# One float32 copy of the first MLP's result between two MLP stages, and a scheduler that counts overwritten inputs

## The chip, the core and the metric

The program runs on one core of a Trainium2 chip. The metric is device microseconds (us) of the whole program, from its start to its end. The engines are named as the profile names them: PE multiplies matrices (PEld loads its weights), DVE, ACT and POOL work on vectors, SP issues the DMAs.

## What is computed

Three layers follow one another. First a gated linear attention with a complex decay, then an MLP with a rational activation, then eight expert MLPs whose outputs are weighted by a Sinkhorn-normalised gate. Only the last result is an output.

```python
x = attention(q, k, v, a_re, a_im)             # 4 x 8 heads x 768 steps x 48, then reshaped to 3072 x 384
h = x @ w_in                                   # first MLP: 384 -> 2048
g = (a0 + a1*h + a2*h*h + a3*h*h*h) / (1 + |b0|*|h| + |b1|*h*h + 1e-6)
x = g @ w_out                                  # 2048 -> 384
P = sinkhorn(exp(x @ w_gate))                  # 3072 x 8
out = sum over e of P[:, e] * (relu(x @ w1[e]) @ w2[e])   # second MLP, 8 experts of 384 -> 1024 -> 384
```

## The kernel before

**Two parts.** In the first part attention and first MLP are interleaved; the page of the profile puts nearly all of it on line 302, where the scheduler issues each operation. In the second part the experts run over the 3072 tokens (PE lines 672 to 674 and 1044 to 1046). A last branch with the general fallback is not taken with these inputs.

**First part.** Attention is cut into 13 pieces (`PIECES`, p = 0 to 12). For each piece `attn_normalise` makes the decays (`n`, `an`), `attn_prefix` the running products (tiles `u`, `tot`, `x`, `f1a`, `f2a`, `ex`; each of four shifts `sh` is a matmul that waits for the `x` before it), `attn_scale` the scaled keys and queries (`f`, `kq`), which go to DRAM (`kqd`) and come back as `raw`. `attn_unit` and `attn_half` then do 24 blocks of 128 tokens on PE (`t`, `sc`, `u`, `y`). The first MLP takes the tokens in 12 blocks of 256 (m = 0 to 11), its 2048 channels in 8 groups (gi): `moe1_first` makes `h` on PE and the activation on ACT and DVE (tiles `m`, result `gt`, or `gh` and `gl`), `moe1_second` adds up `x2` in PSUM.

**Precision by parts.** A float32 matrix product is done as three fast products: a value is split into a rounded part `hi` (type fp32r) and the rest `lo`, and hi*hi, hi*lo and lo*hi are added.

**Between the MLPs.** At the end of a block, `moe1_second` splits `x2` chunk by chunk (three of 128 x 256): ACT (seldom DVE) writes `hi`, DVE writes `lo`, and a DMA of both goes to the DRAM tensor `x2g`. `x2_load` reads 512 tokens of it into a tile `xb` that holds both parts, with one DMA each. Tiles `xb0` to `xb3` take the SBUF space of attention and are loaded when the last block of attention is done; `xb4` and `xb5` are loaded as the second part starts.

**What sets the order.** Every operation is an `Op` with a cost; `Either` lists the engines that may do it (`g.tt`: POOL or DVE; `g.cpa`: ACT, DVE or POOL). The `Schedule` picks, at build time, the operation that could start first by its model, and among those of an engine the one with the lowest key, a due time made of the constants `PITCH`, `GROUP`, `OU`, `OB`, `OA`, `ON`, `OW`, `OS`, `SH`, `HHD`, `WS`. `PRICE` weighs a choice of engine by its cost. An operation with `port` set also waits for a common resource `PORT`: those of POOL with an input in SBUF, and those of DVE with more than one such input. `x is not self.out` leaves an input out of this count where it is also the output. Each engine then works its list in order, so an operation that waits holds up all behind it on its engine.

Of the kernel before, what the change touches and what calls it, by code (L numbers as in the profile page):

```python
# [8 lines left out]
F32 = mybir.dt.float32  # L9
# [9 lines left out]
NT = B * S  # L19
# [42 lines left out]
PLAIN = 'FFFSSFFS'  # L62
SMP = 'DD'

PITCH = 63.96
GROUP = 6.92
OU = 52.54
OB = 77.92
OA = 199.64
ON = 97.15  # L70
OW = 45.47
OS = 27.91
SLACK = 0
HHD = 2.39
SH = (-2.5, 31.7, -15.0, 20.1, 3.1, -26.5, 4.2, 13.7, 4.0, 12.5, -36.2, -58.5, 17.9)
WS = 1.91
PRICE = {'DVE': 1.0, 'POOL': 0.05, 'ACT': -0.18}
LAT = {'PE': 0.2, 'ACT': 0.145, 'DVE': 0.13, 'POOL': 0.075, 'SP': 1.0}
TS = True

# [12 lines left out]
class Op:  # L93


    def __init__(self, eng, fn, args, kw):
        self.eng, self.fn, self.args, self.kw = eng, fn, args, kw
        self.deps = []
        self.out = kw["out"] if "out" in kw else args[0]
        ap = [x for k, x in [*enumerate(args), *kw.items()] if k not in ("out", "accum_out", "op", "func") and hasattr(x, "tensor")]  # L100
        self.ins = [x for x in ap if x is not self.out]
        n = int(np.prod(self.out.shape[1:]))
        ps = any(x.space == PSUM for x in self.ins)
        name = fn.__name__

        sb = sum(x.space != PSUM and int(np.prod(x.shape[1:])) > 1 for x in self.ins)
        self.port = sb > 0 and (eng == "POOL" or eng == "DVE" and (sb > 1 or not ps and name in ("tensor_scalar", "tensor_copy")))
        ptr = sum(hasattr(kw.get(k), "tensor") for k in ("scale", "bias", "accum_out", "scalar")) + (
            name == "tensor_scalar" and sum(hasattr(x, "tensor") for x in args[2:4]))
        self.lat = LAT[eng]  # L110
        if eng == "PE":
            f32 = args[1].dtype != F32R
            two = f32 and not kw.get("is_transpose")
            self.cost = (1 + two) * max(n * (1 + f32) / 2400, 0.108) + 0.013 * (not f32)
            if two:
                self.cost = {32: 0.076, 96: 0.162}.get(self.out.shape[0], self.cost)
        elif eng == "ACT":
            self.cost = (0.05 if ps else 0.092) + n * 0.836e-3 + 0.0935 * ptr
        elif eng == "DVE":
            one = name == "tensor_scalar" and not ps  # L120
            self.cost = ((n / 2 if one else n) + 65) / 960 + 0.061 * ptr
        elif eng == "POOL":
            c = {"tensor_tensor": 2.1, "tensor_scalar": 1.18, "affine_select": 0.9}.get(name, 0.8)
            self.cost = (0.15 if c > 0.8 else 0.04) + c * n * 1e-3
        else:
            self.cost = 0.06
# [709 lines left out]
def moe1_second(g, m):  # L836

    v, act, pool, pe, sync = g.eng
    kw = {"skip_group_check": True}
    for gi in range(NG):  # L840
        yield lambda: (m, gi) in g.gs and (2 * gi, 1) in g.w1 and (2 * gi + 1, 1) in g.w1
        yield m * PITCH + gi * GROUP + OS
        gh, gl = g.gs.pop((m, gi))
        if m not in g.sums:
            g.sums[m] = yield New(g.ps_x, [128, 4, TK], keep=True, tag="x2", name=f"x2_{m}")
        x2 = g.sums[m]
        for f in range(2):
            ff = 2 * gi + f
            w = g.w1[ff, 1]
            for c in range(3):  # L850

                st, sp = ff == 0 and c != 1, ff == NF - 1
                if plain(ff):
                    yield pe.matmul(x2[:, c], w[:, 0, c], gh[:, f], start=st, stop=sp, **kw)
                    continue
                yield [
                    pe.matmul(x2[:, c], w[:, 0, c], gh[:, f], start=st, stop=False, **kw),
                    pe.matmul(x2[:, c], w[:, 1, c], gh[:, f], start=False, stop=False, **kw),
                    pe.matmul(x2[:, c], w[:, 0, c], gl[:, f], start=False, stop=sp, **kw),
                ]  # L860
            if m == NT // TK - 1:
                g.free(w)
        g.free(gh, *([gl] if gl is not None else []))
    for k in range(3):
        x = yield New(g.wraw, [128, 2, TK], F32R, tag="raw", name=f"x2s{m}_{k}")
        sc = g.co[:, 11:12]
        yield Either(act.activation(x[:, 0], x2[:, k], AF.Identity, scale=sc), v.tensor_scalar(x[:, 0], x2[:, k], sc, None, MULT))
        yield v.scalar_tensor_tensor(out=x[:, 1], in0=x2[:, k], scalar=sc, in1=x[:, 0].bitcast(F32), op0=MULT, op1=SUB)
        yield sync.dma_start(
            out=g.x2g[:, k, :, m * TK:(m + 1) * TK].rearrange("l p t -> p l t"), in_=x.bitcast(F32)  # L870
        )
        g.free(x)
    g.free(x2)
    g.done.add(("S", m))

# [364 lines left out]
def general_moe1(g):  # L1240
# [6 lines left out]
    with tc.For_i(0, NT, 128) as t0:  # L1247
        x = tmp.tile([128, DM], F32, tag="gx", name="gx")
        sync.dma_start(out=x, in_=g.yg[bass.ds(t0, 128), :])
        xt = tmp.tile([128, 3, 128], F32, tag="gxt", name="gxt")  # L1250
        for k in range(3):
            p = ps.tile([128, 128], F32, tag="gt", name=f"gtp{k}")
            pe.matmul(p, x[:, k * 128:(k + 1) * 128], g.cst[:, 0], is_transpose=True, start=True, stop=True)
            act.copy(xt[:, k], p)
        acc = [pa.tile([128, 128], F32, tag=f"ga{c}", name=f"ga{c}") for c in range(3)]
        for f in range(NF):
            p = ps.tile([128, 128], F32, tag="gh", name=f"ghp{f}")
            for k in range(3):
                pe.matmul(p, w[2 * f][:, k], xt[:, k], start=k == 0, stop=k == 2)
            h, s, u, z, za, n, d = (tmp.tile([128, 128], F32, tag=f"gm{i}", name=f"gm{i}_{f}") for i in range(7))  # L1260
            act.copy(h, p)
            act.activation(za, p, AF.Abs)
            v.tensor_scalar(s, za, 1.0, None, ALU.max)
            v.reciprocal(u, s)
            v.tensor_tensor(out=z, in0=h, in1=u, op=MULT)
            v.tensor_tensor(out=za, in0=za, in1=u, op=MULT)

            v.tensor_scalar(n, z, co[:, 3:4], None, MULT)
            v.scalar_tensor_tensor(out=n, in0=u, scalar=co[:, 2:3], in1=n, op0=MULT, op1=ADD)
            v.tensor_tensor(out=n, in0=n, in1=z, op=MULT)  # L1270
            v.tensor_tensor(out=d, in0=u, in1=u, op=MULT)
            v.scalar_tensor_tensor(out=n, in0=d, scalar=co[:, 1:2], in1=n, op0=MULT, op1=ADD)
            v.tensor_tensor(out=n, in0=n, in1=z, op=MULT)
            v.tensor_tensor(out=z, in0=d, in1=u, op=MULT)
            v.scalar_tensor_tensor(out=n, in0=z, scalar=co[:, 0:1], in1=n, op0=MULT, op1=ADD)

            v.tensor_scalar(d, d, C1, None, MULT)
            v.tensor_tensor(out=u, in0=u, in1=za, op=MULT)
            v.scalar_tensor_tensor(out=d, in0=u, scalar=co[:, 4:5], in1=d, op0=MULT, op1=ADD)
            v.tensor_tensor(out=za, in0=za, in1=za, op=MULT)  # L1280
            v.scalar_tensor_tensor(out=d, in0=za, scalar=co[:, 5:6], in1=d, op0=MULT, op1=ADD)
            v.reciprocal(d, d)
            v.tensor_tensor(out=n, in0=n, in1=d, op=MULT)
            v.tensor_tensor(out=n, in0=n, in1=s, op=MULT)
            for c in range(3):
                pe.matmul(acc[c], w[2 * f + 1][:, c], n, start=f == 0, stop=f == NF - 1)
        for c in range(3):
            xs = tmp.tile([128, 2, 128], F32R, tag="gxs", name=f"gxs{c}")
            act.copy(xs[:, 0], acc[c])
            v.tensor_tensor(out=xs[:, 1], in0=acc[c], in1=xs[:, 0].bitcast(F32), op=SUB)  # L1290
            sync.dma_start(out=g.x2g[:, c, :, bass.ds(t0, 128)].rearrange("l p t -> p l t"), in_=xs.bitcast(F32))
    g.close("gpa", "gps", "gt", "gm")


def x2_load(g, t):
# [1 line left out]
    per = TB // TK  # L1297
    yield lambda: all(("S", t * per + i) in g.done for i in range(per))
    xt = yield New(g.px[t], [128, 2, 3, TB], F32R, keep=True, tag=f"x{t}", name=f"xb{t}")
    for l in range(2):  # L1300
        yield g.eng[4].dma_start(
            out=xt[:, l].bitcast(F32), in_=g.x2g[l, :, :, t * TB:(t + 1) * TB].rearrange("k p t -> p k t")
        )
    g.x2[t] = xt


# [19 lines left out]
def kernel_body(tc, g):  # L1326
# [22 lines left out]
    dp = opn("dram", space=bass.MemoryType.DRAM)  # L1349
    g.dkq = opn("dkq", 3, space=bass.MemoryType.DRAM)  # L1350
    g.xt = {}
    g.x2g = dp.tile([2, 3, 128, NT], F32, name="x2g")
    g.yg = dp.tile([NT, DM], F32, name="yg")
    g.kq, g.w1, g.we, g.an, g.ex, g.qk, g.gs, g.state, g.carry = ({} for _ in range(9))
    g.done = set()
# [132 lines left out]
```

## Time and profile before

| | |
|---|---|
| median of 3 runs | 2522.71 us (2521.58 to 2524.64) |
| profiled execution | 2521.8 us, of which 2519.8 us is the span from first to last instruction |
| PE busy in the span | 2328.5 us (92%), 13921 matmuls |
| DVE busy | 1201.0 us (48%) |
| ACT busy | 854.1 us (34%) |
| POOL busy | 483.8 us (19%) |
| first matmul of the experts | at 866.7 us |
| granted PE clock over the span | 0.977 of full |

A share over the whole span says little here: the first 867 us and the rest have different limits, and the change lies in the first part and at the seam. Rows are read by stretch.

### The profile page before, as it was taken

To read this page: it belongs to the slowest core of one execution; us is meant where nothing else is said; L and a number is where in the kernel's file an instruction comes from. 1 tells how busy PE (TensorE), PEld (TensorE's weight loads), DVE (VectorE), ACT (ScalarE), POOL (GpSimd) and SP (SyncE) were. 2 spreads that over 40 slices of the span, in tenths; PEclk is the share of its full clock that TensorE was granted. 3 is DMA by queue.
4 is the path that set the end of the run, shared out by engine and by line. 5 is a ranking of instruction groups with operands and counts; after the bars stand their busy time and mean duration, and the time that the engine had idled before them with its cause. 6 is when DMAs were issued, how large, how long until landed. Compare 5 with 4: busy or idle time off the path is not lost.

```text
span 2519.8 us, 34763 instructions
## 1 busy us (share of the span) xinstructions
PE 2328.5 (92%) x13921; PEld 2098.6 (83%) x13921; DVE 1201.0 (48%) x2295; ACT 854.1 (34%) x1741; POOL 483.8 (19%) x537
## 2 busy tenths in 40 slices
PE   1477898988999999999999999999999999999998
PEld 0366788877889978989999989998999999999998
DVE  6899988888987614442252233224222221222222
ACT  3467676766667621221121121121112112112111
POOL 3356444454441000020020020010011002001000
PEclk9888999999999999999999999999999999999999
DMA  3543332333322520030030021012001001000000
GB/s 99 154 126 95 108 107 82 101 90 94 108 89 70 200 64 1 1 94 1 1 100 1 1 71 31 1 39 63 1 13 38 1 1 51 1 1 20 26 25 27
DMA packets 141837, 138.18 MB, mean 55 GB/s; under 512 B 32481, under 2 KB 126689, under 8 KB 141665
## 3 DMA queue, kind: packets, MB, share of 16 engines
q1 hardware_dynamic: 141664, 135.86, 17.7%
q8 instruction: 111, 1.82, 0.3%
q14 instruction: 62, 0.50, 0.1%
HBM read 102.80 MB, written 33.03 MB: 54 GB/s over the span
## 4 chain that ended last, share of the span: by engine, by line
PE 74%; DVE 11%; DMA 6%; issue 3%; POOL 3%; ACT 3%; SPq 1%; POOLq 0%; DVEq 0%; ACTq 0%
PE ye L1044 10%; PE ye L1045 10%; PE ye L1046 10%; PE he L673 10%; PE he L672 10%; PE he L674 10%; PE x L302 4%; DVE m L302 3%; PE h L302 3%; DVE f L302 1%; DMA ai<-in_a_im 1%; ACT m L302 1%; PE t L302 1%; PE sc L302 1%; DVE n L302 1%
## 5 line engine op out<-in xcount | busy, mean ns | idle before, releaser
L1032 DVE SCALAR_TENSOR_TENSOR lo<-he,hi 128x512 fp32r<-128x512 f32 x384 | 265.4, 691 | 1104.5 <-ACT hi L1031 1104.5
L1031 ACT ACTIVATE hi<-he 128x512 fp32r<-128x512 f32 x384 | 229.7, 598 | 1207.6 <-PE he L674 1059.1
L302 DVE SCALAR_TENSOR_TENSOR m<-m,co,m 128x512 f32<-128x512 f32 x192 | 165.5, 894 | 18.7 <-ACT m L302 18.5
L302 ACT ACTIVATE m<-m,co 128x512 f32<-128x512 f32 x192 | 137.4, 719 | 1.4
L302 PE MATMUL t<-cst_sb,raw 128*96 128x128 f32 x384 | 66.5, 304 | 35.6 <-DMA raw<-kqd 33.7
L1057 DVE SCALAR_TENSOR_TENSOR acc<-ye,skp,acc 128x384 f32<-128x384 f32 x168 | 92.2, 611 | 5.7 <-PE ye L1046 2.4
L302 PEld LDWEIGHTS t<-cst_sb,raw 128*96 128x96 f32 x384 | 48.1, 141 | 43.3 <-issue 29.0
L302 DVE SCALAR_TENSOR_TENSOR m<-m,co,h 128x512 f32<-128x512 f32 x96 | 70.7, 738 | 12.9 <-ACT m L302 12.7
L302 ACT ACTIVATE m<-h 128x512 f32<-128x512 f32 x96 | 56.3, 587 | 41.2 <-PE h L302 40.2
L302 PE MATMUL sh<-tot,cst_sb 128*128 128x96 f32 x26 | 8.0, 403 | 64.2 <-POOL tot L302 45.6
L302 ACT COPY tt<-t 96x512 f32<-96x512 f32 x95 | 54.7, 577 | 37.0 <-PE t L302 36.5
L302 ACT ACTIVATE m<-h,co 128x512 f32<-128x512 f32 x96 | 65.3, 680 | 4.2 <-DVE gl L302 1.6
L302 PE MATMUL sc<-tt,tt 96*128 96x128 f32 x384 | 56.2, 291 | 6.0 <-ACT tt L302 5.2
L302 PEld LDWEIGHTS sh<-tot,cst_sb 128*128 128x128 f32 x26 | 5.5, 265 | 66.6 <-POOL tot L302 46.4
L302 ACT ACTIVATE m<-m 128x512 f32<-128x512 f32 x96 | 60.0, 626 | 1.1
L302 PEld LDWEIGHTS sc<-tt,tt 96*128 96x128 f32 x384 | 49.2, 200 | 11.5 <-ACT tt L302 7.7
L302 DVE SCALAR_TENSOR_TENSOR gt<-m,m 128x512 f32<-128x512 f32 x60 | 46.4, 774 | 0.3
L302 ACT ACTIVATE n<-n,bias 128x384 f32<-128x384 f32 x72 | 43.9, 610 | 5.6 <-DVE n L302 3.6
L302 DVE TENSOR_TENSOR f<-an,ex 128x384 f32<-128x384 f32 x70 | 45.5, 665 | 0.0
L302 POOL TENSOR_TENSOR x<-u,u 128x48 f32<-128x48 f32 x62 | 31.6, 526 | 44.6 <-DVE u L302 37.8
L302 POOL TENSOR_TENSOR f<-an,ex 128x384 f32<-128x384 f32 x26 | 32.5, 1256 | 30.7 <-DVE kq L302 10.0
L302 POOL TENSOR_TENSOR kq<-an,f 128x384 f32<-128x384 f32 x21 | 29.9, 1423 | 43.8 <-DVE f L302 26.3
(1329 smaller groups left out, 7018.1 us busy)
## 6 DMA issues: line engine op xcount, KB each, us to landing
rawe<-in_moe_w SPq DMA_DIRECT2D x128, 192.0 KB
kqd<-kq SPq DMA_DIRECT2D x48, 384.0 KB
raw<-kqd SPq DMA_DIRECT2D x48, 384.0 KB
x2g<-x2s SPq DMA_DIRECT2D x36, 256.0 KB
xb<-x2g SPq DMA_DIRECT2D x12, 768.0 KB
raw<-in_moe_w_in SPq DMA_DIRECT2D x48, 128.0 KB
raw<-in_moe_w_out SPq DMA_DIRECT2D x16, 384.0 KB
rawc<-in_moe_w_in SPq DMA_DIRECT2D x16, 384.0 KB
```

The costliest lines, as they stand in the source:

```text
L302: ins = op.fn(*op.args, **op.kw)
L672: pe.matmul(out, w[0], x[0], start=start, stop=False, **kw),
L673: pe.matmul(out, w[0], x[1], start=False, stop=False, **kw),
L674: pe.matmul(out, w[1], x[0], start=False, stop=stop, **kw),
L1031: act.activation(hi, ps, AF.Relu)
L1032: v.scalar_tensor_tensor(out=lo, in0=ps, scalar=0.0, in1=hi.bitcast(F32), op0=ALU.max, op1=SUB)
L1044: pe.matmul(ys[j], hi[:, c], wh, start=f == 0, stop=False)
L1045: pe.matmul(ys[j], hi[:, c], wl, start=False, stop=False)
L1046: pe.matmul(ys[j], lo[:, c], wh, start=False, stop=f == NFE - 1)
L1057: v.scalar_tensor_tensor(out=acc, in0=ys[j], scalar=g.P[:, i, e:e + 1], in1=acc, op0=MULT, op1=ADD)
```

## The change

The block sum `x2` is scaled once into a float32 tile of 128 x 768 by one operation and stored by one DMA of 384 KB; `x2g` has half the size. `x2_load` loads one float32 copy of 768 KB into the `lo` half of the tile, ACT rounds it into the `hi` half (128 x 1536), and POOL or DVE subtracts in place. The count behind `port` takes every input that lies in SBUF, the overwritten ones too. Ten constants of the scheduler have other values, in the list `SH` two entries. The fallback branch is changed in the same way.

```diff
-PITCH = 63.96
-GROUP = 6.92
-OU = 52.54
+PITCH = 63.56
+GROUP = 6.1
+OU = 62.81
...
-OA = 199.64
+OA = 254.69
...
-OW = 45.47
-OS = 27.91
+OW = 55.28
+OS = 26.46
...
-HHD = 2.39
-SH = (-2.5, 31.7, -15.0, 20.1, 3.1, -26.5, 4.2, 13.7, 4.0, 12.5, -36.2, -58.5, 17.9)
-WS = 1.91
-PRICE = {'DVE': 1.0, 'POOL': 0.05, 'ACT': -0.18}
+HHD = 2.09
+SH = (-2.5, 31.7, -15.0, 20.1, 3.1, -26.5, 4.2, 13.7, 9.8, 12.5, -32.7, -58.5, 17.9)
+WS = 2.46
+PRICE = {'DVE': 1.0, 'POOL': 0.12, 'ACT': -0.18}
...
-        sb = sum(x.space != PSUM and int(np.prod(x.shape[1:])) > 1 for x in self.ins)
+        sb = sum(x.space not in (PSUM, DRAM) and int(np.prod(x.shape[1:])) > 1 for x in (ap if "out" in kw else ap[1:]))
...
-    for k in range(3):
-        x = yield New(g.wraw, [128, 2, TK], F32R, tag="raw", name=f"x2s{m}_{k}")
-        sc = g.co[:, 11:12]
-        yield Either(act.activation(x[:, 0], x2[:, k], AF.Identity, scale=sc), v.tensor_scalar(x[:, 0], x2[:, k], sc, None, MULT))
-        yield v.scalar_tensor_tensor(out=x[:, 1], in0=x2[:, k], scalar=sc, in1=x[:, 0].bitcast(F32), op0=MULT, op1=SUB)
-        yield sync.dma_start(
-            out=g.x2g[:, k, :, m * TK:(m + 1) * TK].rearrange("l p t -> p l t"), in_=x.bitcast(F32)
-        )
-        g.free(x)
+    x = yield New(g.wraw, [128, 3, TK], tag="raw", name=f"x2s{m}")
+    sc = g.co[:, 11:12]
+    yield Either(act.activation(x, x2[:, :3], AF.Identity, scale=sc), v.tensor_scalar(x, x2[:, :3], sc, None, MULT))
+    yield sync.dma_start(out=g.x2g[:, :, m * TK:(m + 1) * TK].rearrange("k p t -> p k t"), in_=x)
+    g.free(x)
...
-    for l in range(2):
-        yield g.eng[4].dma_start(
-            out=xt[:, l].bitcast(F32), in_=g.x2g[l, :, :, t * TB:(t + 1) * TB].rearrange("k p t -> p k t")
-        )
+    raw = xt[:, 1].bitcast(F32)
+    yield g.eng[4].dma_start(out=raw, in_=g.x2g[:, :, t * TB:(t + 1) * TB].rearrange("k p t -> p k t"))
+    yield g.eng[1].copy(xt[:, 0], raw)
+    yield g.tt(xt[:, 1], raw, xt[:, 0].bitcast(F32), SUB)
```

The scheduler therefore deals out the first part anew. Counted over its whole list (line 302), POOL has 217 operations where it had 421, DVE 1627 where it had 1471, ACT 1036 where it had 1040. 204 operations leave POOL on balance: 191 of attention and of splits go to DVE, 13 copies to ACT. DVE loses the 38 operations of the split of `x2`, gains 4 subtractions of 128 x 1536, and gives one copy to ACT. By width, the 191 are 47 of 384 columns, 61 of 192, 60 of 48, and 23 of other widths.

The first place is POOL's list at the prefix of piece 6 (`an6` are its decays; `u`, `tot` and `x` its running products), before:

```order
L302 TENSOR_TENSOR u1_6_3562<-an6_2148 128x96
L302 TENSOR_TENSOR u2_6_3563<-an6_2148 128x96
L302 TENSOR_TENSOR tot_6_3538<-u1_6_3562,u2_6_3563 128x48
L302 TENSOR_TENSOR tot_6_3538<-u1_6_3581,u2_6_3582 128x48 x2
L302 TENSOR_TENSOR u1_6_3601<-an6_2148,tot_6_3538 128x96
L302 COPY vtail1_143<-v5_1_3547 128x2x4x16
L302 TENSOR_TENSOR an7_2954<-ar7_0_3397,n3_7_0_3418 128x8x48
L302 TENSOR_TENSOR x_6_3640<-u1_6_3638,u2_6_3639 128x48 x2
L302 COPY gtail0_144<-g5_0_3544 96x2x4x16
L302 TENSOR_TENSOR x_6_3784<-u1_6_3782,u2_6_3783 128x48 x2
```

And POOL's list at the same place now:

```order
L302 TENSOR_TENSOR u1_6_3673<-an6_2077 128x96
L302 TENSOR_TENSOR an7_2858<-ar7_0_3469,n3_7_0_3487 128x8x48
L302 TENSOR_TENSOR x_6_3808<-u1_6_3806,u2_6_3807 128x48 x2
L302 TENSOR_TENSOR n1_7_1_3757<-n1_7_1_3757,n2_7_1_3758 128x384
L302 TENSOR_TENSOR x_6_3895<-u1_6_3893,u2_6_3894 128x48 x2
L302 TENSOR_TENSOR n1_7_1_3757<-n1_7_1_3757,n3_7_1_3759 128x384
```

The running products `tot` and two copies have left POOL, which now has two operations of the next piece's normalisation between the steps of this one.

The second place is DVE's list around the end of block 9 (`x2_9` is its sum, `m1`, `m2` and `gt` are the activation of block 10), before:

```order
L302 SCALAR_TENSOR_TENSOR m2_10_1_8711<-m2_10_1_8711,co_141,h10_1_8676 128x512
L302 SCALAR_TENSOR_TENSOR x2s9_0_8737<-x2_9_8257,co_141,x2s9_0_8737 128x256
L302 SCALAR_TENSOR_TENSOR x2s9_1_8751<-x2_9_8257,co_141,x2s9_1_8751 128x256
L302 SCALAR_TENSOR_TENSOR m1_10_1_8710<-m1_10_1_8710,co_141,m3_10_1_8712 128x512
L302 SCALAR_TENSOR_TENSOR m2_10_1_8711<-m2_10_1_8711,co_141,m3_10_1_8712 128x512
L302 SCALAR_TENSOR_TENSOR x2s9_2_8763<-x2_9_8257,co_141,x2s9_2_8763 128x256
L302 SCALAR_TENSOR_TENSOR gt10_1_8777<-m1_10_1_8710,m2_10_1_8711 128x512
```

And DVE's list there now:

```order
L302 TENSOR_TENSOR kq12_3_8559<-an12_6620,f2_12_8492 128x4x96
L302 SCALAR_TENSOR_TENSOR m1_10_0_8578<-m1_10_0_8578,co_141,m3_10_0_8580 128x512
L302 SCALAR_TENSOR_TENSOR m2_10_0_8579<-m2_10_0_8579,co_141,m3_10_0_8580 128x512
L302 SCALAR_TENSOR_TENSOR m2_10_1_8636<-m2_10_1_8636,co_141,h10_1_8581 128x512
L302 SCALAR_TENSOR_TENSOR gt10_0_8651<-m1_10_0_8578,m2_10_0_8579 128x512
L302 SCALAR_TENSOR_TENSOR m1_10_1_8635<-m1_10_1_8635,co_141,m3_10_1_8637 128x512
L302 SCALAR_TENSOR_TENSOR m2_10_1_8636<-m2_10_1_8636,co_141,m3_10_1_8637 128x512
```

The three splits of the sum are gone, and the last operation of attention's preparation (`kq12_3`) stands here, which before stood in block 9, ahead of `m2_9_6`.

The third place is ACT's list after the last block of attention (`xt11` takes its result, `m1`, `m2` and `m3` are the activation of block 10), before:

```order
L302 ACTIVATE m2_10_6_9070<-h10_6_8902,co_141 128x512
L302 CAST xt11_9007<-y23_9026 128x3x128
L302 ACTIVATE m1_10_6_9069<-m1_10_6_9069,co_141 128x512
L302 ACTIVATE m3_10_6_9071<-m1_10_6_9069,co_141 128x512
L302 ACTIVATE m3_10_6_9071<-m3_10_6_9071 128x512
L302 ACTIVATE m1_10_7_9164,hsum_68<-h10_7_9072 128x512
```

And ACT's list there now:

```order
L302 ACTIVATE m2_10_6_8996<-h10_6_8858,co_141 128x512
L302 CAST xb0_9030<-xb0_9030 128x1536
L302 ACTIVATE m1_10_6_8995<-m1_10_6_8995,co_141 128x512
L302 CAST xb1_9031<-xb1_9031 128x1536
L302 ACTIVATE m3_10_6_8997<-m1_10_6_8995,co_141 128x512
L302 ACTIVATE m1_10_7_9069,hsum_68<-h10_7_8998 128x512
L302 ACTIVATE m3_10_6_8997<-m3_10_6_8997 128x512
L302 ACTIVATE m2_10_7_9070<-h10_7_8998,co_141 128x512
L302 CAST xb2_9032<-xb2_9032 128x1536
L302 ACTIVATE m1_10_7_9069<-m1_10_7_9069,co_141 128x512
L302 CAST xb3_9033<-xb3_9033 128x1536
```

Four roundings of loaded tiles now stand between the steps of the activations of groups 6 and 7; DVE has the four subtractions in two pairs at the same place, the first pair after `gt10_5`, the second after `gt10_6`.

## Rows read from the trace of the kernel before

**Rows 1.** Windows: length, busy us of PE, PEld, DVE, ACT, POOL; clock, DMA share, GB/s.

```profile
0.00:130.00 130.00, 38.68 (x278) 32.72 (x279) 99.41 (x277) 55.06 (x132) 44.96 (x56) 0.90 0.43 125
130.00:755.00 625.00, 534.77 (x4552) 484.94 (x4555) 554.76 (x1066) 416.36 (x903) 311.70 (x355) 0.93 0.34 100
755.00:866.60 111.60, 111.54 (x907) 104.22 (x899) 78.53 (x121) 83.16 (x163) 13.27 (x14) 1.00 0.36 118
...
818.00:838.00 20.00, 20.00 (x145) 18.92 (x138) 10.32 (x15) 10.93 (x21) 0.00 (x0) 1.00 0.89 315
```

**Rows 2.** Waits from 130 to 755 us: total, times, longest.

```profile
PE t L302 <- DMA raw<-kqd: 12.1, 7, 2.9
...
PE sh L302 <- POOL tot L302: 7.4, 4, 3.4
...
PE sh L302 <- POOL x L302: 4.0, 3, 2.5
```

**Rows 3.** DVE groups to 880 us: count, busy us, mean ns, idle before.

```profile
L302 DVE SCALAR_TENSOR_TENSOR m<-m,co,m 128x512 f32<-128x512 f32 x192 | 165.5, 894 | 18.7 <-ACT m L302 18.5
L302 DVE SCALAR_TENSOR_TENSOR m<-m,co,h 128x512 f32<-128x512 f32 x96 | 70.7, 738 | 12.9 <-ACT m L302 12.7
...
L302 DVE TENSOR_TENSOR f<-an,ex 128x384 f32<-128x384 f32 x70 | 45.5, 665 | 0.0
L302 DVE SCALAR_TENSOR_TENSOR n<-n,n 128x384 f32<-128x384 f32 x48 | 35.5, 739 | 0.1
...
L302 DVE SCALAR_TENSOR_TENSOR x2s<-x,co,x2s 128x256 fp32r<-128x256 f32 x36 | 17.2, 476 | 6.9 <-ACT x2s L302 6.9
```

**Rows 4.** The same by tile: shortest/median/longest ns, first and last start.

```profile
L302 DVE SCALAR_TENSOR_TENSOR m<-m,co,m x192: 734/750/1776, 128.9 to 866.7; 128x512 f32<-128x512 f32 x192
L302 DVE SCALAR_TENSOR_TENSOR m<-m,co,h x96: 729/736/749, 126.5 to 863.1; 128x512 f32<-128x512 f32 x96
...
L302 DVE TENSOR_TENSOR f<-an,ex x70: 543/548/1639, 49.5 to 758.6; 128x384 f32<-128x384 f32 x70
...
L302 DVE TENSOR_TENSOR an<-f,f x54: 343/346/1152, 50.8 to 759.6; 128x192 f32<-128x192 f32 x54
...
L302 DVE SCALAR_TENSOR_TENSOR n<-n,n x48: 541/552/1364, 17.2 to 691.3; 128x384 f32<-128x384 f32 x48
...
L302 DVE TENSOR_TENSOR tot<-u,u x44: 192/201/1025, 51.7 to 723.6; 128x48 f32<-128x48 f32 x44
```

**Rows 5.** POOL groups to 880 us.

```profile
L302 POOL TENSOR_TENSOR an<-f,f 128x192 f32<-128x192 f32 x42 | 32.9, 787 | 22.4 <-DVE f L302 22.3
...
L302 POOL TENSOR_TENSOR x<-u,u 128x48 f32<-128x48 f32 x62 | 31.6, 526 | 44.6 <-DVE u L302 37.8 <-PE t L302 6.8
L302 POOL TENSOR_TENSOR kq<-an,f 128x384 f32<-128x384 f32 x21 | 29.9, 1423 | 43.8 <-DVE f L302 26.3 <-issue 14.8 <-ACT f L302 2.6
L302 POOL TENSOR_TENSOR an<-f1a,f2a 128x192 f32<-128x192 f32 x30 | 26.9, 905 | 25.9 <-DVE f1a L302 25.6
```

**Rows 6.** Timeline of DVE from 870.9 us: start, us, what.

```profile
871.00 0.55 DVE L302 TENSOR_TENSOR we4o<-rawe,we4o 128x384 fp32r<-128x384 f32 x1
871.47 0.55 DVE L302 TENSOR_TENSOR we5i<-rawe,we5i 128x384 fp32r<-128x384 f32 x1
```

**Rows 7.** Timeline of ACT from 877 us.

```profile
879.88 0.51 ACT L302 CAST we6o<-rawe 128x384 fp32r<-128x384 f32 x1
```

**Rows 8.** Timeline of SP's DMA issues from 760 us.

```profile
818.37 10.08 SPq L302 DMA_DIRECT2D xb<-x2g  x8
```

**Rows 9.** Longest pieces of the chain that ended last: start, us, what.

```profile
306.11 6.61 DMA raw<-kqd
...
772.61 6.91 PE x L302 x48
779.52 2.15 PE h L302 x18
781.67 2.59 PE x L302 x12
```

More of the change, by code (lines that the diff above doesn't have):

```diff
@@ L1287, in general_moe1 @@
         for c in range(3):
[L1288 to L1291, printed above, removed]
+            xs = tmp.tile([128, 128], F32, tag="gxs", name=f"gxs{c}")
+            act.copy(xs, acc[c])
+            sync.dma_start(out=g.x2g[c, :, bass.ds(t0, 128)], in_=xs)
     g.close("gpa", "gps", "gt", "gm")
@@ L1351, in kernel_body @@
     g.xt = {}
-    g.x2g = dp.tile([2, 3, 128, NT], F32, name="x2g")
+    g.x2g = dp.tile([3, 128, NT], F32, name="x2g")
     g.yg = dp.tile([NT, DM], F32, name="yg")
```

## The prediction

> **What bounds the kernel now.** I read the windows first, because the change lies in the first 867 us alone. They show two stretches with different limits [rows 1]. From 130 to 755 us nothing is full: of 625 us DVE is busy 554.8 (89%), PE 534.8 (86%), ACT 416.4, POOL 311.7. From 755 us to the first matmul of the experts PE is busy 111.54 of 111.6 us, DVE 78.5. So the second stretch is a sum of matmuls, and every stall of PE there adds to the time; the first is paced by DVE and by chains that pass through it. The experts behind are PE's work too and keep their program. The waits of the first stretch name DVE and POOL ahead of PE in attention's prefix: its shift matmuls wait 7.4 us for `tot` from POOL and 4.0 for `x` from POOL; transposes wait 12.1 us for loads of `kqd`, which the change doesn't touch [rows 2].
>
> Then I compare DVE's groups by mean and by median, because DVE's 89% is not all work. `m<-m,co,m`, with both tensor inputs in SBUF, takes 894 ns in the mean, 750 in the median and 1776 at most; `m<-m,co,h`, which reads one from PSUM, has the same width and never takes more than 749 [rows 3, 4]. In both of the SBUF-only groups that show it beside it, `n` and `f`, the median is near the shortest and the mean far above it. Some executions of these are stretched, and POOL is what works beside them. The stretch is (894 - 750) x 192 = 27.6 us for `m`, (739 - 552) x 48 = 9.0 for `n`, (665 - 548) x 70 = 8.2 for `f`: 45 us in three groups [rows 3, 4]. The smaller groups, reckoned in the same way, add about 53: some 98 us that DVE loses beside POOL.
>
> **The change, part by part.**
>
> *What DVE gains.* 191 operations come over from POOL. On DVE a 384-wide one lasts 0.55 us, but the next starts 0.47 after it [rows 6], so a place in the list costs 0.08 less than a duration. 47 of 384 columns: 22.1 us. 61 of 192, at 0.346 - 0.08 [rows 4]: 16.2. 60 of 48, at 0.201 - 0.08 [rows 4]: 7.3. The 23 of other widths lie between these, about 0.25 each: 5.8. Together 51 us.
>
> *What DVE loses.* The split's 36 operations of 17.2 us in all [rows 3]; nine of the twelve blocks end before 755 us, so three quarters of it, 12.9 us, fall there. That DVE and ACT no longer take turns over three chunks frees `x2` some 2 us earlier per block, which I count at nothing: PE has other products in its list.
>
> *What POOL's leaving gives back.* Four groups carry most of it [rows 5]: 17 `kq<-an,f` of 1.423 us, 45 `x` of 0.526, 24 `an<-f1a,f2a` of 0.905, 27 `an<-f,f` of 0.787 make 91 us. The other 91 of the 204 I take at 0.8, the mean of these 113: 73. So about 164 of the 357 us that POOL works before 755 (311.7 and 45.0 ahead of 130 [rows 1]) go away, 46%. No row shows DVE beside a POOL half as busy. The floor is that only the three groups above are relieved, 46% of 45 = 21 us; the ceiling is that the new list keeps what is left of POOL clear of DVE, 98 us. I take 46% of 98 = 45, because the loss goes with the time that POOL works: it is absent where an input is in PSUM and where POOL rests.
>
> *Sum for DVE:* 51 - 13 - 45 = -7 us, between +17 and -60. DVE is 89% busy there, so I let it pass one to one.
>
> *Chains.* Half of the 11.4 us in which PE's shifts wait for POOL [rows 2] should go, as `tot` leaves POOL and `x` mostly does (45 of 62). Each step idles DVE too, which waits for the shift. Part of this is in the sum already, so I take -4, between 0 and -8.
>
> *Scheduler.* The constants and the wider `port` decide only the order, and their price is in the counts above. DVE's list reaches the end of attention's preparation (`kq12_3`) some two groups later than before, while the first matmul of attention's last two blocks keeps its place in PE's list, behind the first product of `gt10_0`. PE's products of block 10 ahead of that are the cover; if it were gone, each us that `kq12_3` is late would be one at the end.
>
> *The seam.* Stores and loads halve: SP issues 24 stores and 6 loads fewer, all off the path. New is that ACT rounds `xb0` to `xb3` in the middle of block 10's last two activations, and that each rounding waits for a load. A 1536-wide rounding costs at most four of 384 columns, 2.0 us [rows 7], I take 1.5; a subtraction on DVE at most four of 0.47, 1.9. ACT and DVE are half idle there (10.9 and 10.3 us of 20) [rows 1], so the work fits; the wait is the risk, because ACT and DVE hold `gt10_6` and `gh10_7` behind it, and PE wants those. Before, the first load is issued at 818.4 [rows 8], as attention's last matmul ends. PE then has 12 products of `gt10_2`, 18 of `h10_7` and 48 of groups 3 to 5: 2.59 + 2.15 + 6.91 = 11.7 us [rows 9], so it asks for `gt10_6` at about 830, and for `gh10_7` 4.7 us later. The loads moved 315 GB/s [rows 1]: 0.79 MB is 2.5 us, and no landing is shorter; a load of half the size kept PE's chain 6.6 us [rows 9]. With 4.5 us the first lands at 823. From there ACT needs two roundings and three activations (5 us), DVE two subtractions and four products of the activation (about 6, partly beside it): `gt10_6` at 831.5, some 2 us late, and `gh10_7`, behind two more roundings, another 1 to 2. The price is 3 us, between 0 (2.5 us to land) and 6 (6.6). A rule that bears on it, on the Trainium skill's page "DMA: Bandwidth & Descriptors", section "Anatomy of one DMA", puts a DMA at 2.0 us and its bytes over 436 GB/s, measured on another path of issue; an estimate from that page is 3.8 us for this load, and a seam of 2 us instead of 3. No row of this trace shows the landing of `xb0` by itself.
>
> `xb4` and `xb5` are subtracted on POOL, at four times the shortest 384-wide POOL operations or more, 4 us each and more. Nothing on PE's way waits for them: the gate wants `xb4` some 40 us later.
>
> By the Trainium skill, page "SBUF — State Buffer", section "Who interferes with whom", DVE and GpSimd share one pair of ports under an exclusive lock, so one of them stands still for the whole instruction of the other. The longest `m<-m,co,m` agrees with it: 1776 against 734 ns is one POOL instruction of about 1 us [rows 4]. By this rule the subtractions of `xb4` and `xb5` would each stop DVE's splits of weights for 4 us, a loss that the old kernel doesn't have; DVE's `lo` of the experts reads PSUM and goes on, so the sum stays.
>
> **Total.** 2521.8 us for the profiled execution - 7 - 4 + 3 = 2513.8, and with the first 130 us, where the prefix's first `tot` also leaves POOL, -1: 2512.8. The median of the runs is 0.9 us above the profiled one: I say 2513.
>
> **Rivals.**
>
> *DVE loses more than it gets (slower).* It is the engine nearest to full, and 38 us net come onto it before any relief. If what is left of POOL meets DVE more often, since DVE's list is denser, the relief stays at 21 us, and DVE takes 17 more: 2521.8 + 17 + 3 - 2 = 2540. It decides from a relief under about 35 us, with a chance of 0.25. For it speaks that POOL's parts are not spread evenly: long 384-wide operations stay there; against it, that the chains lose their hops.
>
> *No change.* DVE is relieved, but PE's stretch is held by the loads of `kqd` (12.1 us) and by chains through ACT, and what is won ahead of 755 is waited for again: 2519 to 2526. For it speaks that no engine is above 89%; chance 0.17.
>
> *The new order fits better.* If the list now stands in the order in which things are ready, PE's 90 idle us of the first stretch (625 - 534.8) could fall by a third beyond the sum, with a relief near its ceiling: about 2485. Chance 0.15.
>
> *The forecast,* between 2500 and 2517: 0.43.
>
> **How the numbers follow.** About 0.2% (5 us) is what this measurement can tell from no change. Faster is the forecast and the better order, 0.58; same 0.17; slower 0.25. The range leaves out the far ends of the last two: 2485 to 2537; the likeliest case alone is 2500 to 2517.
>
> **What the new profile would show.** In the stretch up to 755 us POOL at about 170 us and DVE still near 89%; `m<-m,co,m` near 820 ns in the mean with an unchanged median; the waits of `sh` for POOL halved; the tail full but for about 3 us near 830, named as `x` waiting for `gt` or `gh`; the first matmul of the experts at about 858 us. The prediction is wrong if DVE's mean durations don't fall with POOL's time, or if PE waits for an `xb` load for more than 6 us.

## The result and the profile after

The changed kernel takes 2485.38 us (median of 4 runs, 2481.61 to 2488.16), the kernel before 2522.14 beside it: a ratio of 0.9858, with a 95% interval of 0.9838 to 0.9879. The profiled execution has a span of 2486.4 us; the four runs lie in two pairs, near 2482 and 2488 us, and it belongs to the slower one, so the profiles show 33 of the 37 us. The kernel is faster by 37 us where I had said 10, and the likeliest case alone was 2500 to 2517, so the size was wrong. That 2485.38 still lies in the range from 2485 to 2537, by 0.4 us, is luck.

The experts start at 834.2 us where they started at 866.7, and take 1652.2 us from there as against 1653.1. So the gain is in the first part. These are the windows after, with the columns of [rows 1]; the last row is the whole first part:

```profile
0.00:130.00 130.00, 43.94 (x303) 37.76 (x304) 96.10 (x283) 53.13 (x129) 33.06 (x45) 0.89 0.43 126
130.00:755.00 625.00, 554.30 (x4791) 507.72 (x4790) 573.07 (x1259) 443.12 (x952) 168.81 (x171) 0.95 0.33 98
755.00:866.60 111.60, 109.60 (x806) 98.05 (x805) 67.16 (x108) 76.50 (x143) 17.40 (x14) 0.98 0.36 115
...
0.00:834.20 834.20, 675.44 (x5728) 616.92 (x5729) 725.38 (x1622) 557.42 (x1195) 206.21 (x220) 0.94 0.34 102
```

And the whole first part of the kernel before, in the same view:

```profile
0.00:866.70 866.70, 685.09 (x5729) 621.96 (x5729) 732.80 (x1463) 554.57 (x1197) 369.94 (x424) 0.93 0.35 106
```

An engine's busy time and its idle time add up to the length of the part. DVE's busy time falls by 7.4 us, from 732.80 to 725.38: near the sum that I had made for it, -7, though it holds the four subtractions of the seam (6.9 us), which I had not put into that sum. Its idle time falls by 25.1, from 133.9 to 108.8, for which I had 4. Without the seam, up to the end of attention's last block on DVE, the two windows are these, after and before; DVE's busy time falls by 13.6 us there and its idle time by 23.5:

```profile
0.00:782.70 782.70, 625.94 (x5396) 570.51 (x5397) 686.91 (x1569) 516.11 (x1121) 202.48 (x217) 0.94 0.34 101
```

```profile
0.00:819.80 819.80, 638.22 (x5400) 577.43 (x5401) 700.54 (x1414) 519.22 (x1128) 363.72 (x419) 0.93 0.34 102
```

Seen from PE over the whole first part, the same 5729 products take 9.65 us less, at a granted clock of 0.94 where it was 0.93, and 22.8 us of idle time go.

DVE's groups after, as [rows 3], then the same by tile, as [rows 4]:

```profile
L302 DVE SCALAR_TENSOR_TENSOR m<-m,co,m 128x512 f32<-128x512 f32 x192 | 150.1, 801 | 11.7 <-ACT m L302 11.4
L302 DVE SCALAR_TENSOR_TENSOR m<-m,co,h 128x512 f32<-128x512 f32 x96 | 70.4, 739 | 7.4 <-ACT m L302 7.2
...
L302 DVE TENSOR_TENSOR f<-an,ex 128x384 f32<-128x384 f32 x74 | 41.7, 580 | 0.0
...
L302 DVE SCALAR_TENSOR_TENSOR n<-n,n 128x384 f32<-128x384 f32 x48 | 28.0, 582 | 0.0
```

```profile
L302 DVE SCALAR_TENSOR_TENSOR m<-m,co,m x192: 734/745/1575, 126.6 to 833.4; 128x512 f32<-128x512 f32 x192
```

The mean of `m<-m,co,m` falls from 894 to 801 ns with a median of 745 where it was 750, `f` from 665 to 580, `n` from 739 to 582; `m<-m,co,h`, with one input in PSUM, stays (738 and 739). That is the relief, where I looked for it.

PE's waits from 130 to 755 us, as [rows 2]:

```profile
PE x L302 <- DVE gt L302: 15.2, 7, 4.6
PE h L302 <- DVE m L302: 14.5, 6, 7.4
PE h L302 <- ACT w15i L302: 8.8, 1, 8.8
PE t L302 <- DMA raw<-kqd: 7.9, 5, 2.7
PE sh L302 <- DVE x L302: 6.3, 6, 2.1
```

No row of `sh` waiting for POOL is left in this stretch; the loads of `kqd` cost 7.9 us where they cost 12.1.

**What I had not looked at.** I took the waits for POOL from PE's view alone. From 120 us to the experts the rows for POOL in the views of PE, DVE and ACT add up to 15.3, 10.0 and 31.7 us before, and to 0.7, 0.4 and 4.0 after. The largest of them, from ACT's view of the kernel before (total, times, longest):

```profile
ACT f L302 <- POOL an L302: 19.9, 9, 5.6
```

One place of the kernel before shows how such a wait comes about and goes on: first POOL's timeline from 469 us, then DVE's from 469.7, then PE's from 481.

```profile
469.85 3.41 POOL L302 TENSOR_TENSOR kq<-an,f 128x384 f32<-128x384 f32 x1 [2.26 <-DVE f L302]
473.21 1.02 POOL L302 TENSOR_TENSOR f2a<-an 128x384 f32<-128x384 f32 x1
```

```profile
469.69 0.69 DVE L302 SCALAR_TENSOR_TENSOR m<-m,m 128x512 f32<-128x512 f32 x1
470.29 0.55 DVE L302 TENSOR_TENSOR n<-n,n 128x384 f32<-128x384 f32 x1
470.76 0.55 DVE L302 SCALAR_TENSOR_TENSOR n<-n,n 128x384 f32<-128x384 f32 x1
471.23 0.55 DVE L302 TENSOR_TENSOR f1a<-an 128x384 f32<-128x384 f32 x1
471.69 0.69 DVE L302 TENSOR_TENSOR gl<-m,gh 128x512 fp32r<-128x512 f32 x1
474.27 0.36 DVE L302 TENSOR_TENSOR an<-f1a,f2a 128x192 f32<-128x192 f32 x1 [1.89 <-POOL f2a L302]
474.54 0.55 DVE L302 SCALAR_TENSOR_TENSOR n<-n,n 128x384 f32<-128x384 f32 x1
475.01 0.35 DVE L302 TENSOR_TENSOR an<-f1a,f2a 128x192 f32<-128x192 f32 x1
475.28 0.74 DVE L302 SCALAR_TENSOR_TENSOR m<-m,co,h 128x512 f32<-128x512 f32 x1
```

```profile
481.23 0.98 PE L302 MATMUL h<-xt,w6i 128*128 128x256 f32 x6 [2.25 <-DVE m L302]
```

POOL's `kq` lasts 3.41 us, and its next operation 1.02 at the same width: it is held as long as DVE works without a pause on operations with two inputs in SBUF, and ends 0.9 us after the last of them, `gl`, at 472.38. DVE then has nothing but `an` at the head of its list, which wants POOL's `f2a`, and idles 1.89 us; its product of the activation stands behind that, and 6 us later PE waits 2.25 us for the next of these products. So the two engines hold each other up in both directions, and the loss is idle time of DVE, ACT and PE beside the stretched instructions that I had added up. The Trainium skill's page "SBUF — State Buffer", section "Who interferes with whom", says of the ports that the two share that whoever comes first has them for a whole instruction, and the other stands still. These rows agree in that POOL stands still; they show it for longer than one instruction, through five of DVE's in a row.

### The profile page after: what moved, and what is told of

Its sections match the earlier page's. It is cut to its first block, busy times and chain, and to the rows that moved or that the text cites. A ratio compares the mean times of both kernels' runs of the same rounds, so it can differ in the third digit from the quotient of the medians.

```text
span 2486.4 us, 34564 instructions
## 1 busy us (share of the span) xinstructions
PE 2318.9 (93%) x13921; PEld 2093.5 (84%) x13921; DVE 1191.3 (48%) x2451; ACT 859.6 (35%) x1739; POOL 327.0 (13%) x335
## 4 chain that ended last, share of the span: by engine, by line
PE 75%; DVE 12%; DMA 6%; ACT 3%; issue 2%; SPq 1%; POOL 1%; DVEq 0%; POOLq 0%; ACTq 0%
PE ye L1040 11%; PE ye L1041 11%; PE ye L1042 10%; PE he L673 10%; PE he L672 10%; PE he L674 10%; PE h L302 4%; DVE m L302 3%; PE x L302 3%; DVE f L302 2%; DMA ai<-in_a_im 2%; ACT m L302 1%; PE sc L302 1%; PE t L302 1%; DVE an L302 1%
## 5 line engine op out<-in xcount | busy, mean ns | idle before, releaser
L302 DVE SCALAR_TENSOR_TENSOR m<-m,co,m 128x512 f32<-128x512 f32 x192 | 150.1, 801 | 11.7 <-ACT m L302 11.4
L302 ACT COPY tt<-t 96x512 f32<-96x512 f32 x96 | 55.3, 576 | 23.4 <-PE t L302 22.8
L302 POOL TENSOR_TENSOR n<-n,n 128x384 f32<-128x384 f32 x22 | 28.9, 1313 | 83.7 <-ACT n L302 83.7
L302 DVE TENSOR_TENSOR sm<-sc,cst_sb 128x512 f32<-128x512 f32 x48 | 32.8, 683 | 12.4 <-PE sc L302 12.3
```

The lines of the kernel that those rows point to most:

```text
L302: ins = op.fn(*op.args, **op.kw)
```

## The experiments

Each ran beside the kernel before on the same chip, whose median was 2518.2 us for the first and third four and 2516.2 for the second. First a table of all, worked out from the windows from 0 to each kernel's first matmul of the experts: idle is the length less the busy time. "Copy" is the block sum as one float32, "count" the new count behind `port`, "table" the new due times and POOL's price of 0.12.

| kernel | copy, count, table | POOL us (instructions) | DVE busy / idle | PE idle | experts at | ratio, interval |
|---|---|---|---|---|---|---|
| before | none | 369.9 (424) | 732.8 / 133.9 | 181.6 | 866.7 | 1 |
| only_table | table | 360.4 (381) | 737.0 / 118.3 | 179.7 | 855.3 | 0.9973, 0.9961 to 0.9984 |
| only_x2 | copy | 373.9 (424) | 728.8 / 126.6 | 174.1 | 855.4 | 0.9971, 0.9958 to 0.9984 |
| no_port | copy, table | 350.6 (376) | 726.5 / 137.4 | 183.4 | 863.9 | 1.0023, 1.0014 to 1.0033 |
| only_port | count | 208.2 (240) | 731.7 / 126.9 | 180.6 | 858.6 | 0.9967, 0.9955 to 0.9978 |
| no_x2 | count, table | 194.0 (234) | 727.9 / 113.5 | 167.5 | 841.3 | 0.9933, 0.9916 to 0.9949 |
| newcount_more | all, POOL cheaper | 282.5 (260) | 722.7 / 133.8 | 173.3 | 856.5 | 0.9963, 0.9951 to 0.9976 |
| oldcount_dear | copy, table, POOL dearer | 237.3 (249) | 719.5 / 119.3 | 166.1 | 838.8 | 0.9904, 0.9888 to 0.9921 |
| changed kernel | all | 206.2 (220) | 725.4 / 108.8 | 158.8 | 834.2 | 0.9858, 0.9838 to 0.9879 |
| no_table | copy, count | 201.2 (220) | 733.4 / 100.3 | 163.2 | 833.6 | 0.9885, 0.9861 to 0.9908 |
| jit_ow | all, `OW` 54.3 | 198.1 (214) | 720.4 / 120.3 | 165.0 | 840.7 | 0.9921, 0.9901 to 0.9941 |
| jit_group | all, `GROUP` 6.2 | 189.3 (215) | 720.1 / 122.7 | 163.8 | 842.8 | 0.9874, 0.9857 to 0.9890 |
| newcount_less | all, POOL dearer | 130.4 (147) | 728.6 / 115.7 | 160.7 | 844.3 | 0.9924, 0.9907 to 0.9940 |
| seam_late | all, roundings later | 209.9 (220) | 726.6 / 98.3 | 156.4 | 824.9 | 0.9851, 0.9835 to 0.9868 |

**One part at a time.** Only the count, in the kernel before:

```diff
-        sb = sum(x.space != PSUM and int(np.prod(x.shape[1:])) > 1 for x in self.ins)
+        sb = sum(x.space not in (PSUM, DRAM) and int(np.prod(x.shape[1:])) > 1 for x in (ap if "out" in kw else ap[1:]))
```

> The kernel before with only the new count behind `port`; POOL's list is 238 operations long where it was 421. Pace (DVE's busy time sets the end, as the prediction has it): 51 us come onto DVE, 45 are given back, the chains give 4: 2520, with DVE's idle time as before. Chains (operations on POOL are slow links in which DVE and PE wait; with them gone DVE idles less): about 2495, with DVE's idle time ahead of the experts some 25 us shorter. Table (the due times do it): 2522 or more.

Measured 2512.51 us. POOL's list shrinks as in the full change, which shows that it is the count, and not the table, that takes the operations from POOL. The gain is small: DVE's busy time stays (-1.1), its idle time falls by 7. Yet DVE's instructions are relieved as in the full change, and its waits for ACT in the activation are the 31.0 us that they were before (up to 860 us):

```profile
L302 DVE SCALAR_TENSOR_TENSOR m<-m,co,m 128x512 f32<-128x512 f32 x192 | 147.6, 787 | 13.5 <-ACT m L302 13.1
```

```profile
DVE m L302 <- ACT m L302: 31.0, 29, 3.5
```

PE's idle time stays too (180.6 us, 181.6 before).

Only the copy, with the edits of `moe1_second` and `x2_load`:

```diff
-    for k in range(3):
-        x = yield New(g.wraw, [128, 2, TK], F32R, tag="raw", name=f"x2s{m}_{k}")
...
+    x = yield New(g.wraw, [128, 3, TK], tag="raw", name=f"x2s{m}")
```

> The kernel before with only the float32 copy of the block sum; POOL keeps 421 operations. Pace: 12.9 us less on DVE, 3 us more at the seam: 2512. Chains and table: the splits stand where DVE waits anyway, so 2518 to 2523.

Measured 2511.63, as the pace has it, though in another way: DVE's busy time falls by 4.0 and its idle time by 7.3.

Only the table:

```diff
-PITCH = 63.96
-GROUP = 6.92
+PITCH = 63.56
+GROUP = 6.1
...
-PRICE = {'DVE': 1.0, 'POOL': 0.05, 'ACT': -0.18}
+PRICE = {'DVE': 1.0, 'POOL': 0.12, 'ACT': -0.18}
```

> The kernel before with only the new due times and the price of POOL; POOL keeps 380 of 421 operations. Pace: 10 us onto DVE, about as much given back: 2522. Chains: 2522, less at most a tenth of the gain for the tenth of POOL's operations that go: 2518. Table: about 2490.

Measured 2512.52, some 6 us less than the kernel before, which no theory had; the whole gain can't rest on it. DVE's idle time falls by 15.6 us here although POOL is nearly as busy as before (360.4 us), so a fall of it alone is no sign of POOL's leaving.

**All but one part.** The changed kernel with the old count:

```diff
-        sb = sum(x.space not in (PSUM, DRAM) and int(np.prod(x.shape[1:])) > 1 for x in (ap if "out" in kw else ap[1:]))
+        sb = sum(x.space != PSUM and int(np.prod(x.shape[1:])) > 1 for x in self.ins)
```

> The changed kernel with the old count behind `port`; POOL has 374 operations. Pace: 2512 (the block sum's 12.9 us less on DVE, 3 us at the seam). Chains: 2515 or more, most of the gain lost. Table: about 2488, as the changed kernel.

Measured 2525.08: all of the gain is lost, and more, as only the theory of the chains had it. The pace missed it by 13 us. (Its experts also take some 6 us longer from their start, 2522.6 - 863.9 us. PE's waits are 2.7 us of it, 4.3 as against the 1.6 of the changed kernel; the rest stays open.)

The changed kernel with the old path of the block sum (the copy's edits undone):

> The changed kernel with the old path of the block sum (three splits per block, both parts stored and loaded); POOL has 231 operations. If the parts of the change add up as their single runs did (0.33% for the count, 0.27% for the table, 0.29% for the copy), this is 2518 - 15 = 2503. If the gain belongs to the count and the table together, with the copy worth its 0.3%: 2492. If each version's gain is the luck of its order: anywhere from 2490 to 2520, as the next runs scatter.

Measured 2500.64, or 0.9933, about what the parts add up to.

The changed kernel with the old due times and price:

> The changed kernel with the old due times and the old price of POOL; POOL has 217 operations as in the changed kernel. If the parts add up: 2518 - 16 = 2502. If the count needs its table: 2505 or more, near the count alone. If the table does nothing: 2485.

Measured 2487.72, beside the changed kernel: with the count and the copy the table is worth about 0.3% (0.9885 and 0.9858, whose intervals overlap), and the rival that saw the gain in a better order by the new due times falls.

**The scatter of the order.** Two kernels change one due time of the changed kernel by 2%, which deals out the first part anew:

```diff
-OW = 55.28
+OW = 54.3
```

> The changed kernel with `OW` at 54.3 where it was 55.28, a change of 2% that only deals out the first part anew (POOL 211 operations). If the count and the copy set the time, within 5 us of the changed kernel: 2480 to 2490. If the changed kernel's order is a lucky one: 2495 to 2510.

```diff
-GROUP = 6.1
+GROUP = 6.2
```

> The changed kernel with `GROUP` at 6.2 where it was 6.1 (POOL 212 operations). The same: 2480 to 2490 if the parts of the change set the time, 2495 to 2510 if it is this one order.

Measured 2496.75 and 2486.66. The first is as far off as I had said for a lucky order, the second is not off at all. So an order of the same parts by itself is worth 10 us and more, and a single pair of kernels can't price a part to less than about 0.3%, the standard deviation of the three ratios 0.9858, 0.9921 and 0.9874.

**Does POOL's leaving pay, or the plan's knowledge?** The new count does both: it takes work from POOL, and it lets the scheduler plan POOL and DVE apart. Here POOL leaves by its price, under the old count:

```diff
-        sb = sum(x.space not in (PSUM, DRAM) and int(np.prod(x.shape[1:])) > 1 for x in (ap if "out" in kw else ap[1:]))
+        sb = sum(x.space != PSUM and int(np.prod(x.shape[1:])) > 1 for x in self.ins)
...
-PRICE = {'DVE': 1.0, 'POOL': 0.12, 'ACT': -0.18}
+PRICE = {'DVE': 1.0, 'POOL': 0.8, 'ACT': -0.18}
```

> The changed kernel with the old count behind `port`, and POOL's price at 0.8 where it was 0.12, so that POOL leaves by its price: it has about 245 operations (374 with the old count at the old price, 217 in the changed kernel). The plan still holds that an operation which overwrites its input leaves POOL free. If POOL's leaving is what pays (less work beside DVE, shorter chains): 0.988 of the kernel before, as the four kernels that have both the new count and the copy (0.986 to 0.992), and DVE's idle time ahead of the experts near 110 us. If it pays that the plan knows what POOL and DVE keep from each other: 0.998 or more, with DVE's idle time near 130.

Measured 2495.33, 0.9904: nearer what POOL's leaving would give (0.988) than what the plan's knowledge would (0.998), while DVE's idle time, 119.3 us, lies midway. Against `no_port`, from which only the price differs, that is 1.2% less. DVE has 125 instructions more in the first part of `oldcount_dear` than in that of `no_port`, and is yet busy 7 us less and idle 18 us less. First the first part of `no_port`, its `m<-m,co,m` and DVE's wait for ACT in the activation (up to 860 us), then those of `oldcount_dear`:

```profile
0.00:863.90 863.90, 680.49 (x5716) 618.16 (x5717) 726.48 (x1467) 552.82 (x1183) 350.64 (x376) 0.94 0.33 98
```

```profile
L302 DVE SCALAR_TENSOR_TENSOR m<-m,co,m 128x512 f32<-128x512 f32 x192 | 162.4, 877 | 18.7 <-ACT m L302 18.6
```

```profile
DVE m L302 <- ACT m L302: 48.3, 36, 5.6
```

```profile
0.00:838.80 838.80, 672.69 (x5717) 612.02 (x5718) 719.54 (x1592) 554.61 (x1188) 237.34 (x249) 0.94 0.33 101
```

```profile
L302 DVE SCALAR_TENSOR_TENSOR m<-m,co,m 128x512 f32<-128x512 f32 x192 | 148.9, 804 | 17.7 <-ACT m L302 17.4
```

```profile
DVE m L302 <- ACT m L302: 29.6, 28, 4.4
```

These waits fall from 48.3 to 29.6 us between the two (31.0 and 18.6 before and after the change), while the rows for POOL in the three views stay, 28.6 and 31.8 us together. So with POOL's leaving DVE's instructions run nearer their own speed (804 ns where it was 877), and in this pair the chain through ACT, DVE and PE turns faster as well; the direct waits for POOL are not the larger part. The faster instructions are not enough by themselves, as `only_port` shows, where the chain kept its waits. What the knowledge adds is within the scatter of the order.

The other way, the count as in the change, with POOL's price lower, and higher:

```diff
-PRICE = {'DVE': 1.0, 'POOL': 0.12, 'ACT': -0.18}
+PRICE = {'DVE': 1.0, 'POOL': -0.02, 'ACT': -0.18}
```

> The changed kernel with POOL's price at -0.02: the count is new, and POOL has some 40 operations more (257, with a third more work by the scheduler's costs). If POOL's leaving pays: a fifth to a third of the way back, 0.990 to 0.993. If the plan's knowledge pays: 0.988, as the others with the new count.

```diff
-PRICE = {'DVE': 1.0, 'POOL': 0.12, 'ACT': -0.18}
+PRICE = {'DVE': 1.0, 'POOL': 0.6, 'ACT': -0.18}
```

> The changed kernel with POOL's price at 0.6: POOL has 143 operations, a third less. If POOL's leaving pays: 0.982 to 0.985, DVE's stretched time falling with POOL's. If the plan's knowledge pays: 0.986 to 0.992; DVE's busy time comes out even, as in the change.

Measured 2509.15 and 2499.07. The first has only 40 instructions more on POOL, but 76 us more work (282.5 against 206.2), which is 47% of what had left; 0.9963 is about three quarters of the way back, more than I had allowed, and against the plan's knowledge, which had 0.988. The second misses my figure the other way: with POOL at 130 us nothing more is won, and 0.9924 is what the plan's knowledge had, so it speaks for neither rival alone. DVE is busy 3 us more than in the changed kernel (what it takes over is no longer paid back), and PE's products take 8 us longer.

**The seam.** In the changed kernel ACT's timeline from 782 us and PE's from 792 us:

```profile
782.75 0.68 ACT L302 ACTIVATE m<-h,co 128x512 f32<-128x512 f32 x1
787.63 1.47 ACT L302 CAST xb<-xb 128x1536 fp32r<-128x1536 f32 x1 [4.19 <-issue]
789.01 0.72 ACT L302 ACTIVATE m<-m,co 128x512 f32<-128x512 f32 x1
789.83 1.48 ACT L302 CAST xb<-xb 128x1536 fp32r<-128x1536 f32 x1
```

```profile
792.33 1.46 PE L302 MATMUL x<-gt,w11o 128*128 128x256 f32 x6
795.78 2.50 PE L302 MATMUL x<-gt,w12o 128*128 128x256 f32 x6 [2.00 <-DVE gt L302]
798.08 2.25 PE L302 MATMUL x<-gt,w13o 128*128 128x256 f32 x6
```

The loads were issued from 781.75. ACT comes to the first rounding at 783.4 and idles 4.19 us (the row names no releaser; that it was the load, I read from the order of the lists); the activation stands behind it, and PE waits 2.00 us for `gt10_6`. Then six products take 2.50 and 2.25 us where they took 1.46. In the windows the clock is 0.62 from 795.80, and full before and behind:

```profile
790.00:793.70 3.70, 3.70 (x22) 3.12 (x21) 3.25 (x3) 3.70 (x7) 0.00 (x0) 1.00 0.55 205
795.80:800.30 4.50, 4.50 (x14) 3.65 (x15) 4.50 (x4) 2.39 (x3) 0.00 (x0) 0.62 0.00 0
800.30:804.00 3.70, 3.70 (x32) 3.60 (x31) 1.67 (x4) 2.11 (x5) 0.00 (x0) 1.00 0.02 4
```

So the lower of the clock's two levels, 1.2 GHz, was granted for most of the 4.5 us behind the wait. The last experiment holds the roundings back:

```diff
     yield g.eng[4].dma_start(out=raw, in_=g.x2g[:, :, t * TB:(t + 1) * TB].rearrange("k p t -> p k t"))
+    if t < 4:
+        yield lambda: (10, 7) in g.gs
     yield g.eng[1].copy(xt[:, 0], raw)
```

> The changed kernel with the roundings of `xb0` to `xb3` held until `gh10_7` is planned; the lists are the same up to there. By my account of the seam: the wait of `x` for `gt` near 795 us (2.0 us) goes, and the experts start 2 us earlier, 2483. If the wait only moves (to `gh10_7`, or to the experts' first `xb0`): no change, or up to 3 us later.

Measured 2480.29 (2478.51 to 2482.62), a ratio of 0.9851 to the kernel before: its interval and the changed kernel's overlap, so the whole time doesn't settle it. The stretch does: from the end of attention's last block on DVE (776.0 us, and 782.7 in the changed kernel) to the experts it takes 48.9 us as against 51.5 (46.9 in the kernel before), and the granted clock stays full. First the changed kernel, then `seam_late`:

```profile
782.70:834.20 51.50, 49.50 (x334) 46.41 (x333) 38.47 (x54) 41.31 (x76) 3.73 (x3) 0.97 0.31 103
```

```profile
776.00:824.90 48.90, 47.65 (x335) 45.35 (x333) 39.79 (x54) 41.89 (x77) 3.23 (x3) 1.00 0.34 113
```

PE's waits of `seam_late` from 760 to 830 us are one row:

```profile
PE h L302 <- DVE m L302: 1.3, 1, 1.3
```

The wait for `gt` is gone, a shorter one for `m` came instead. The ratio is the lowest of all that ran, though within the scatter between orders.

## Why the prediction was right in its direction and too small

- **DVE's sum** was about right: -7 forecast, -7.4 measured with the seam's subtractions in it, -13.6 up to the end of attention's last block. The copy takes 17.2 us [rows 3] and brings 6.9 (four subtractions of 1.756 us), 10.3 net; with the 51 us that I had counted for the operations that came over, the relief works out as 51 - 10.3 + 7.4 = 48 us, where I had 45. The trace agrees: the mean less the median, times the count, comes to 106 us over all of DVE's groups before (I had 98) and to 59 after, 47 less. That the share of 46% held in the sum (47 of 106 is 44%) is partly luck, since it didn't hold by groups: `m<-m,co,m`, `n` and `f` lose 30 of their 45 us, all others 17 of 61.
- **The step that failed** is the one behind it, "I let it pass one to one", with the term "Chains" at -4: up to the end of attention's last block 23.5 us of DVE's idle time went, beside 13.6 us of its busy time. The term was taken from PE's waits for POOL alone, half of 11.4 us [rows 2], when ACT waited 31.7 us for POOL and DVE 10.0. And it saw a stretched instruction as a loss of its own length only. That the operations' leaving makes the idle time fall, `no_port` and `oldcount_dear` show (18 us of DVE's, 17 of PE's), both with the copy; without it, in `only_port`, it was 7 and 1. That it comes about by a faster chain of the activation is read from DVE's waits for ACT, and is not shown apart.
- **PE's clock** had no term. The same products took 9.65 us less of PE's time, with a granted clock of 0.94 where it was 0.93. This is part of the 32.5 us, not beside DVE's account.
- **The seam** was +3 (0 to 6): 51.5 - 46.9 = 4.6 us, of which 2.0 are the wait, named as I had said, and 2.50 + 2.25 - 2 x 1.46 = 1.8 the clock behind it, which I had not counted. The first `xb`, issued with three more, could be read 5.9 us after its issue, above my 4.5 and inside my bounds. The estimate of 3.8 us, from the Trainium skill's page "DMA: Bandwidth & Descriptors", section "Anatomy of one DMA", was for one load by itself; this trace has four at once and doesn't show it.
- **The first 130 us** were forecast at -1. The first block's sum is stored at 233.4 us (226.2 before), the ninth's at 699.3 (743.7): the gain comes between them, and not ahead.
- **POOL's work** from 130 to 755 us is 168.8 us, as forecast (170). DVE is busy 92% of it, not "near 89%": the line by which I said the forecast could be judged shows that its idle time went.
- **The rivals.** "The new order fits better" named 2485, and that is the time, but its reason holds only in part. It wanted a third of PE's 90 idle us from 130 to 755 to go, and 19.5 went (90.2 to 70.7). It also wanted a relief near 98 us, which is 47, and without the new due times the kernel is nearly as fast (0.9885). "DVE loses more than it gets" needed a relief under 35. "No change" fell by PE's idle time.
- **`xb4` and `xb5`** on POOL take 3.52 and 3.51 us, not "4 and more"; DVE's splits of the weights had been done ahead of them, and its `lo` beside the first, which reads PSUM, took 0.68 us. The loss that the rule of the ports gave there did not occur in this order. The longest `m<-m,co,m` before stood beside a `gl` of POOL of 1.68 us that had begun 0.45 us ahead of it, and not beside one of about 1 us.

**What stays open.** The six kernels with the copy and under 240 us of work on POOL (`seam_late` aside) have ratios of 0.9858 to 0.9924, 0.9894 in the mean: 1.06%, some 27 us, are what such orders give on average, the other 9 us belong to this one. Of the 27, the parts alone explain less: the two kernels with little work on POOL and no copy have 0.9967 and 0.9933, the two with the copy and much work on POOL 0.9971 and 1.0023, the two with neither 1 and 0.9973; by their means, one would expect 0.996 of both together. In pairs, the count gives 0.86% and 1.65% where the copy is there (`only_x2` to `no_table`, `no_port` to the changed kernel), and 0.33% and 0.40% where it is not. That the two help each other (the splits of the sum waited for ACT for 5.2 and 8.2 us in `only_port` and `no_x2`, and 6.9 [rows 3] before) is likely, but with a scatter of 0.3% between orders these runs don't settle how much.

## What to carry to other kernels

Work that is moved between two engines which share something is priced by three sums and not by one: what comes over, what is no longer stretched, and the waits of every engine for the slower one, ACT's and DVE's own among them, since an engine that waits also holds up what stands behind it in its list. Here the fall of idle time was larger than that of busy time, 23.5 as against 13.6 us. Where a program orders the work, try the same parts in two or three neighbouring orders before a difference of 0.3% is put down to a part. An engine to which work was given because it was idle can cost the others more time than it saves them. There can also be a point beyond which taking more from it gives nothing: here, as far as single orders show it, between 280 and 200 us of the first part's 840.

## What the runs showed of the hardware that was not expected

- An operation of POOL can be held far longer than one of DVE: `kq<-an,f` of 128 x 384 took 3.41 us beside a DVE that did not pause, and 995 ns at the shortest; the longest of DVE in the same kernel was 1.776 us for 0.734. In the changed kernel an `f<-an,ex` of POOL, 128 x 384 too, took 5.75 us from 580.39 us, beside a DVE without a pause.
- A wait of PE of 2.0 us cost 3.8: behind it the granted clock was 0.62 over 4.5 us, though PE had been busy at full clock up to it.
- The same lists differ from one execution to another: up to the seam `seam_late` has the changed kernel's order, and came to the end of attention at 776.0 us where the changed kernel's profiled execution came at 782.7.
